# Tile-by-tile gather for the first expert, one-hot masks on ScalarE, two weight pieces decoded later

## The chip, the cores and the metric

The kernel runs on one core of one Trainium2 chip. The metric is device microseconds of one execution, the median of several runs. The engines are TensorE (PE in the profile, its weight loads PEld), VectorE (DVE), ScalarE (ACT), GpSimd (POOL) and SyncE (SP), whose queue issues nearly all DMAs.

## The reference

Three computations follow each other. The attention hashes queries and keys into 64 buckets by the signs of a projection on 6 columns, and masks pairs of different buckets. Its result, 1536 tokens of 512 numbers, goes to the one expert of eight with the highest logit. A last layer has a wide hidden vector of 1024 numbers, a softmax gate, a normalisation and an output product.

```python
mask = q_bucket[:, :, :, None] == k_bucket[:, :, None, :]
scores = np.where(mask, scale * np.matmul(q, k.transpose(0, 1, 3, 2)), -1000000000.0)
attn_out = softmax(scores) @ v                       # 2 x 8 heads x 768 x 64
x = attn_out as 1536 tokens x 512
e_idx = np.argmax(x @ w_gate, axis=1)
for e in range(8):
    ye = np.maximum(x[e_idx == e] @ w1[e], 0.0) @ w2[e]
    out[e_idx == e] = gate_w * eom * ye
h = out @ w_in; solu = h * softmax(h)
return normalise(solu) * g_ln @ w_out
```

`w_in` and `w_out` of the last layer arrive as 64-bit floats. The kernel reads them as pairs of 32-bit words and puts 32-bit floats together from these on the chip; this is called decoding here.

## The kernel before, in words

**Attention.** The order of instructions on each engine is the order in which the program emits them; nothing reorders it afterwards. 96 units of 128 queries x 768 keys pass through PE (scores), DVE (maximum), ACT (exponential), PE (transposes, product with v). Sixteen blocks `j` of three token tiles end in `fin_hi`, `fin_lo` (split of the result into two 16-bit halves), `fin_r` (reciprocal of the sums), `fin_mm` (PE: transposition and router logits), `fin_l` (logits to SBUF) and `fin_x` (tokens as two 16-bit halves `xh`; the second half of the split is on POOL, or on DVE for tile 11). L1028 to L1037 emit the units, and work in the background hangs on them by `at` and `due`.

**Routing.** Twelve token tiles are routed in five parts (L747): tiles 0 to 2, 3 to 5, 6 to 8, 9 and 10, and 11. `route_a` (L752, DVE) makes a one-hot row of the chosen expert for each token, `route_mm` (L771, PE) counts with small matmuls how many tokens of the same expert came before, `route_b` (L790) writes each token's slot `slot_f` on DVE and issues one indirect DMA per tile on POOL's queue, which scatters the tile's tokens into `xs` in DRAM. `route_s` (L810) adds the part's counts to `hs` on DVE, which the matmuls of later parts and of `totals` read.

**The gather for expert 0.** The other experts' tokens come back from `xs` by a transposing DMA (`x_load`, L1095). For expert 0 the tokens of tiles 0 to 5 are loaded so early (`gather_load`, L901), and the rest is put in by matmuls: `gather_first` (L925) writes the loaded rows into four PSUM tiles, `gather_oh` (L917) makes a mask of 128 x 224 per token tile on DVE (1 where the token's slot is the column), and `gather_mm` (L929) multiplies the tile's tokens by the mask, 8 matmuls per tile, six tiles. `gather_copy` (L937) moves the four PSUM tiles to SBUF with four copies on ACT. The order of all of this at the end of attention is written out by hand in L1040 to L1082; before, all six masks follow after the last parts are routed:

```python
for t in (6, 7, 8):
    oh(t)
    gm(t, range(4))
a_("route_b")(4)
for t in (9, 10, 11):
    oh(t)
    gm(t, range(4))
```

`totals` (L848) starts with one matmul of `hs`, ahead of the first expert's matmuls on PE, and goes on with a long series of small DVE operations that orders the experts by their number of tokens; from its `slot_i` SP reads into registers which weights to load (`expert`, L1212), and ACT and DVE read where results go. `route_d` (L819) makes the gate weights.

**Experts.** 64 slots of four per product (L1225 and on): `mm1` and `mm2` of eight experts with 24 matmuls each. `ev1` and `ev2` split a slot's result into a high half (ACT) and a low half (DVE, put off by one slot through `late`). A slot also has one piece of weights to split: ACT the high half (L167), DVE the low half (L171), with loads three slots ahead (`LA`) into five buffers `raw`. PSUM has eight buffers here, so PE can run some slots ahead of DVE.

**Decoding.** `w_in` and `w_out` are 16 pieces of 128 x 512. A piece takes a load (`wide_load`, L115), `wide_abs` on ACT, `wide_clamp` on POOL (L130), `wide_a`, `wide_c`, `wide_b` on DVE (L135, L141, L146), `wide_hi` on POOL (L152), `wide_lo` on DVE (L171). Pieces 0 to 2 are decoded during attention; the list `WD` (L1247) gives the slot at which each of pieces 3 to 15 starts, its load six slots before. In the list of before, piece 14 starts at slot 47 and piece 15 at 64, which is the first slot of the last stage.

**Last stage.** For token tile t = 0 to 11: `h2` (24 matmuls), `solu_a` to `solu_d` (softmax, normalisation, split, transposing DMA), and, from t = 4 on, `outp(t - 4)` (24 matmuls with `w_out`, then a scatter to the output). The work of slots 64 + 2t and 65 + 2t is emitted at the head of tile t.

Of the kernel before, what the change touches and what calls it, by code (L numbers as in the profile page):

```python
# [21 lines left out]
def kernel(  # L22
# [75 lines left out]
    win = const.tile([1, 4], I32, name="win")  # L98
    g1 = const.tile([128, KF], F32, name="g1")
    nhalf = const.tile([128, 1], F32, name="nhalf")  # L100


    wide = w_in.dtype == I64
# [155 lines left out]
    def setup_late():  # L259
        ie = const.tile([128, E], I32, name="ie")  # L260
        it = const.tile([128, B, NS], I32, name="it")
        g = nc.gpsimd
        g.memset(rg, 0.0)
        for h in range(2):
            r = slice(64 * h, 64 * h + 64)
            for wi, w in enumerate((w_gate, w_ogate)):
                c0 = 128 + 16 * h + 8 * wi
                nc.sync.dma_start(out=rg[r, :, c0 - 128:c0 - 120],
                                  in_=w.rearrange("(c h p) e -> h p c e", h=2, p=64)[h])
        nc.sync.dma_start(out=g1, in_=g_ln.rearrange("(f p) -> p f", p=128))  # L270
        g.iota(ie, pattern=[[1, E]], base=0, channel_multiplier=0)
        g.iota(it, pattern=[[S, B], [1, NS]], base=0, channel_multiplier=NS)
        make_upper_triangular(nc, upper, val=1.0, diag=False)
        g.memset(ones16, 1.0)
        g.memset(nhalf, -0.5)
        g.tensor_copy(out=iota8, in_=ie)
        g.tensor_copy(out=me[:, :, 1], in_=it.rearrange("p b s -> p (b s)"))
        g.tensor_scalar(out=iota_s, in0=iota8, scalar1=1.0 / 16.0, scalar2=1.0, op0=ALU.mult, op1=ALU.mult)
        g.tensor_scalar(out=ord0, in0=iota8, scalar1=-1.0, scalar2=1.0, op0=ALU.mult, op1=ALU.mult)
        for e in range(2):  # L280
            g.memset(ord0[:, e:e + 1], float(16 * NT * (2 - e)))
        for e in range(E):
            g.memset(caps[:, e:e + 1], float(CAPS[e]))
        for x in range(MW):
            g.memset(win_w[:, x:x + 1], float(WIN * x))
        g.tensor_scalar(out=row0, in0=iota8, scalar1=float(NT), scalar2=1.0, op0=ALU.mult, op1=ALU.mult)

        g.memset(hs, 0.0)
        g.tensor_scalar(out=hs[:, 0], in0=iota8, scalar1=float(NT // 128), scalar2=1.0, op0=ALU.mult, op1=ALU.mult)
# [20 lines left out]
    def attention(es):  # L310
# [603 lines left out]
                                    op0=ALU.add, op1=ALU.mult)  # L914
            gx["xe"], gx["oh"] = xe, bh

        def gather_oh(t):  # L917
            nc.vector.tensor_scalar(out=gx["oh"][:, t - 6], in0=gx["oh"][:, 6], scalar1=slot_f[:, t:t + 1],
                                    scalar2=None, op0=ALU.is_equal)

        def gather_ps():
            a = ps_s.tile([128, 2, 512], F32, tag="s", name="s")
# [13 lines left out]

        def gather_copy():  # L937
            xw = raw.tile([128, 1024], F32, tag="raw", name="raw").bitcast(F16)[:, 0:8 * CAP]
            xw = gx["xw"] = xw.rearrange("p (c n) -> p c n", c=8)
            for kk in range(4):  # L940
                nc.scalar.copy(out=xw[:, kk::4], in_=gx["ps"][kk][:, 0:2 * CAP].rearrange("p (a n) -> p a n", a=2))

        JL = 2 * NP - 2
        for n in range(1, NP):
# [66 lines left out]
    with tc.manual_schedule():  # L1011
        with ExitStack() as es:
            A = attention(es)
            pj = A["pj"]
            cm, rb, rg = A["cm"], A["rb"], A["rg"]
            setup_first()
            A["first"]()
            A["load"](1)
            setup_late()
            NU = A["NU"]  # L1020
            bg = A["bg"]
            JL = 2 * NP - 2
            a_ = A.__getitem__
            pv, fa, tr = a_("emit_pv"), a_("fin_a"), a_("emit_t")
            due = a_("due")
            J = JL + 1
            for i in range(NU):
                a_("emit_s")(i, a_("steps_t")(i - 2) if 2 <= i else iter(()))  # L1028
                due(i, 0)
                a_("emit_max")(i)  # L1030
                due(i, 1)
                if i == NU - 1:
                    tr(NU - 2)
                a_("emit_exp")(i)
                if i == 5 or i >= 6 and i % 2 == 0:
                    pv(i // 2 - 2)
                due(i, 2)  # L1037
            assert not bg, bg.keys()

            oh, gm = a_("gather_oh"), a_("gather_mm")  # L1040
            pv(NU // 2 - 2)
            a_("fin_l")(JL)
            a_("fin_x")(JL)
            a_("fin_r")(J, 0, 2)
            a_("fin_hi")(J, 0, 2, True)
            tr(NU - 1)
            a_("fin_lo")(J, 0, 2)
            a_("fin_mm")(J, 0, 2)
            a_("route_a")(2)
            pv(NU // 2 - 1)  # L1050
            a_("fin_hi")(J, 2, 3, True)
            a_("fin_l")(J, 0, 2)
            a_("fin_x")(J, 0, 2, True)
            a_("route_a")(3)
            a_("fin_lo")(J, 2, 3)
            a_("fin_r")(J, 2, 3)
            a_("gather_ps")()
            a_("gather_first")(range(4))
            a_("fin_mm")(J, 2, 3)
            a_("route_mm")(2, tail=True)  # L1060
            a_("route_b")(2)
            a_("fin_l")(J, 2, 3)
            a_("route_s")(2)
            a_("route_a")(4)
            a_("fin_x")(J, 2, 3, True, True)
            a_("route_mm")(3, tail=True)
            a_("route_b")(3)
            a_("route_mm")(4, (9, 10), True)
            for t in (6, 7, 8):
                oh(t)  # L1070
                gm(t, range(4))
            a_("route_b")(4)
            for t in (9, 10, 11):
                oh(t)
                gm(t, range(4))
            a_("gather_copy")()
            a_("route_s")(3)
            for x in range(3):
                a_("route_d")(x, 0, 1)
            a_("totals")()  # L1080
            for x in range(3):
                a_("route_d")(x, 2, 3, 4)  # L1082
# [12 lines left out]
        def x_load(e, r0, w=CAP):  # L1095
            xw = mp.tile([128, 2 * KD, CAP], F16, tag="xw", name="xw", bufs=3)
            x = nc.sync.dma_start_transpose(out=xw[:, :, 0:w], in_=xs[r0, :])
            xw_t[e] = xw
            if e in (1, "x"):
                for y in scattered:  # L1100
                    tc.add_manual_dep(x.ins, y.name, mybir.DependencyInfo(
# [55 lines left out]

        def mm1(e, g, n):
            w = wt["w1", e].rearrange("p a (k f) -> p a k f", k=KD)
            xw = xw_t[e][:, :, 0:n]  # L1160
            if g == 0:
                hh_t[e] = mp.tile([128, 2, KF, CAP], F16, tag="hh", name="hh")
            ps = ps_a.tile([128, 2, CAP], F32, tag="a", name="a")
            for i in range(2):
                fs = slice((2 * g + i) * 128, (2 * g + i + 1) * 128)
                for kk in range(KD):
                    nc.tensor.matmul(ps[:, i, 0:n], w[:, 0, kk, fs], xw[:, kk], start=(kk == 0), stop=False)  # L1167
                    nc.tensor.matmul(ps[:, i, 0:n], w[:, 0, kk, fs], xw[:, KD + kk], start=False, stop=False)  # L1168
                    nc.tensor.matmul(ps[:, i, 0:n], w[:, 1, kk, fs], xw[:, kk], start=False, stop=(kk == KD - 1))  # L1169
            return ps  # L1170

        def ev1(e, g, ps, n):
# [71 lines left out]
                f(*a)  # L1244


        WD = [0, 2, 6, 10, 14, 18, 22, 27, 32, 37, 42, 47, 64]  # L1247
        for x in range(16):
            if wide:
                if x < EARLY:  # L1250
# [206 lines left out]
```

## Time and profile before

| what | us |
|---|---|
| three runs, median (lowest to highest) | 526.81 (526.65 to 527.11) |
| the profiled execution, its own time | 526.2 |
| the profiled execution, its span | 524.4 |
| PE busy in the span | 501.5 (96%) |
| DVE busy | 389.5 (74%) |
| ACT busy | 317.4 (61%) |
| POOL busy | 283.2 (54%) |

The span runs from the first to the last instruction; 1.8 us of the profiled execution's own time lie outside it. Attention takes the span up to some 236 us, routing and gather to 251, the experts to 388, the last stage to the end. PE is busy nearly throughout, so what counts is where it waits or runs at its lower clock. In the timeline a row gives start, duration, engine, line and operation, the tile written and the tiles read, and in brackets how long the engine sat idle before it and what it waited for. A row "x4" stands for four like instructions.

### The profile page before, as it was taken

How to read it: one execution, taken by the hardware profiler on the slowest of the kernel's cores; microseconds unless marked ns; L12 is line 12 of the kernel's file. 1: busy time of each engine (PE TensorE's matmuls, PEld its weight loads, DVE VectorE, ACT ScalarE, POOL GpSimd, SP SyncE). 2: the span in 40 equal slices, each digit the busy share in tenths (PEclk: the TensorE clock that was granted, in tenths of full speed). 3: DMA queues.
4: the chain of work that ended last, by engine and by line, in shares of the span. 5: the costliest groups of instructions: out<-in, count | busy, mean ns of one | idle time of the engine just before them, and what ended most of it. 6: DMA issues, size and time to landing. Idle time of an engine off the chain costs nothing. (4 is left out here: it accounts for less than half of the span.)

```text
span 524.4 us, 12447 instructions
## 1 busy us (share of the span) xinstructions
PE 501.5 (96%) x4692; PEld 384.7 (73%) x4692; DVE 389.5 (74%) x926; ACT 317.4 (61%) x595; POOL 283.2 (54%) x433
## 2 busy tenths in 40 slices
PE   7799999999999999997999999999979999999994
PEld 4578787888787888886999999999854444444442
DVE  7788888888888888766489898969934887455610
ACT  5778787888778887881364665566612455334420
POOL 7999896969879796826166587212111012212131
PEclk9999999999999999998999999999999999999998
DMA  5678988763837675302699999998500236352250
GB/s 180 144 201 188 243 151 236 194 184 86 201 115 126 200 174 167 78 2 81 194 288 227 314 307 296 272 313 279 173 5 0 55 76 112 80 96 66 61 140 40
DMA packets 107183, 83.23 MB, mean 159 GB/s; under 512 B 80624, under 2 KB 89456, under 8 KB 107120
## 3 DMA queue, kind: packets, MB, share of 16 engines
q1 hardware_dynamic: 104816, 76.09, 57.8%
q0 software_dynamic: 2304, 6.31, 3.1%
q8 instruction: 38, 0.62, 0.5%
q14 instruction: 25, 0.20, 0.1%
HBM read 51.43 MB, written 9.97 MB: 117 GB/s over the span
## 5 line engine op out<-in xcount | busy, mean ns | idle before, releaser
L627 PE MATMUL t<-ident,p 128*128 128x128 f32 x576 | 126.1, 275 | 0.5
L615 ACT ACTIVATE p<-s,mx 128x768 f32<-128x768 f32 x96 | 95.7, 997 | 38.7 <-DVE mx L604 22.4
L600 DVE TENSOR_REDUCE mx<-s 128x1 f32<-128x768 f32 x96 | 91.6, 955 | 27.0 <-PE s L590 21.6
L629 ACT COPY pt<-t 128x384 f32<-128x384 f32 x192 | 85.5, 479 | 7.0 <-PE t L627 5.8
L627 PEld LDWEIGHTS t<-ident,p 128*128 128x128 f32 x576 | 77.8, 141 | 15.4 <-ACT pt L629 8.9
L651 PE MATMUL v<-pt,v 128*64 128x128 f32 x1128 | 72.0, 277 | 0.0
L1323 PE MATMUL h<-wi,yT 128*128 128x512 f16 x288 | 65.2, 386 | 2.9 <-PEq L1127 2.9
L651 PEld LDWEIGHTS v<-pt,v 128*64 128x64 f32 x1128 | 60.6, 137 | 7.8 <-issue 6.8
L1197 PE MATMUL a<-hh,wb 128*128 128x224 f16 (+5 forms) x256 | 63.4, 251 | 2.0 <-DVE hh L1176 1.9
L1391 PE MATMUL o<-wo,zT 128*128 128x512 f16 x288 | 63.6, 379 | 0.1
L130 POOL TENSOR_SCALAR dm<-dm 128x512 f32<-128x512 f32 x16 | 33.2, 2072 | 56.4 <-ACT dm L125 56.2
L1196 PE MATMUL a<-hh,wb 128*128 128x224 f16 (+5 forms) x256 | 63.4, 251 | 0.0
L1198 PE MATMUL a<-hh,wb 128*128 128x224 f16 (+5 forms) x256 | 63.4, 251 | 0.0
L590 PE MATMUL s<-k,q 128*128 128x384 f16 x192 | 59.0, 329 | 1.0 <-ACT p L615 1.0
L590 PE MATMUL s<-b,cm 128*128 128x384 f16 x192 | 57.2, 326 | 1.4 <-DVE b L552 1.4
L1323 PEld LDWEIGHTS <-yT 128*128 128x128 f16 x288 | 28.6, 99 | 38.0 <-issue 5.4
L1167 PE MATMUL a<-xw,wa 128*128 128x224 f16 (+5 forms) x224 | 55.2, 249 | 0.3 <-DVE hh L1176 0.3
L1169 PE MATMUL a<-xw,wa 128*128 128x224 f16 (+5 forms) x224 | 55.2, 249 | 0.0
L1168 PE MATMUL a<-xw,wa 128*128 128x224 f16 (+5 forms) x224 | 55.2, 249 | 0.0
L1391 PEld LDWEIGHTS <-zT 128*128 128x128 f16 x288 | 28.2, 98 | 34.3 <-issue 0.4
L1401 POOL DMA_INDIRECT out_dram<-o,tok x12 | 12.6, 1047 | 53.8 <-issue 46.9
L1339 ACT ACTIVATE ex<-h,st,csc 128x1024 f32<-128x1024 f32 x12 | 14.4, 1203 | 41.8 <-DVE st L1362 27.6
(269 smaller groups left out, 1031.4 us busy)
## 6 DMA issues: line engine op xcount, KB each, us to landing
raw<-in_moe_w_dram SPq DMA_DIRECT2D x64, 512.0 KB, 6.1
raww<-in_moe_w_in_dram SPq DMA_DIRECT2D x8, 512.0 KB
raww<-in_moe_w_out_dram SPq DMA_DIRECT2D x8, 512.0 KB
xs<-raw SPq DMA_DIRECT2D x8, 448.0 KB, 4.0
v<-in_v_dram SPq DMA_DIRECT2D x8, 384.0 KB
q<-in_q_dram SPq DMA_DIRECT2D x6, 384.0 KB
k<-in_k_dram SPq DMA_DIRECT2D x6, 384.0 KB, 5.6
cm<-q SPq DMA_DIRECT2D x14, 96.0 KB, 2.1
```

Source lines behind the costliest of these rows:

```text
L590: nc.tensor.matmul(t[:, c, 0:SB], d[x, h][:, s], flat(d[y, h])[:, c * SB:(c + 1) * SB], start=first, stop=not first)
L600: nc.vector.tensor_reduce(out=mx[:, 0:1], in_=t[:, :, 0:SB], op=ALU.max, axis=AX.XY)
L615: nc.scalar.activation(out=p, in_=s_t.pop(i)[:, :, 0:SB], func=AF.Exp, scale=mx[:, 1:2], bias=mx[:, 2:3], accum_out=sums[j][:, qt, h:h + 1])
L627: nc.tensor.transpose(t[:, g * 128:(g + 1) * 128], p[:, c, g * 128:(g + 1) * 128], ident)
L629: nc.scalar.copy(out=pt[i][:, 3 * c:3 * c + 3], in_=t[:, 0:SB].rearrange("p (g c) -> p g c", g=3))
L651: nc.tensor.matmul(o[64 * h:64 * h + 64], vt[:, h, c], ph[h][:, c], start=(c == 0), stop=(c == NS - 1), tile_position=(0, 64 * h))
L1167: nc.tensor.matmul(ps[:, i, 0:n], w[:, 0, kk, fs], xw[:, kk], start=(kk == 0), stop=False)
L1196: nc.tensor.matmul(ps, w[:, 0, f, ds], hh[:, 0, f], start=(f == 0), stop=False)
L1197: nc.tensor.matmul(ps, w[:, 0, f, ds], hh[:, 1, f], start=False, stop=False)
L1198: nc.tensor.matmul(ps, w[:, 1, f, ds], hh[:, 0, f], start=False, stop=(f == KF - 1))
L1323: nc.tensor.matmul(ps[:, c], yT[:, a, kk, ts], w_i[:, w, kk, c * 512:(c + 1) * 512], start=(kk == 0 and a == 0 and w == 0), stop=(kk == KD ...
L1391: nc.tensor.matmul(ps, zT[:, KF * a + f], w_o[:, w, f], start=(f == 0 and a == 0 and w == 0), stop=(f == KF - 1 and a == 1))
```

## The change

Five things are changed. (1) The hand-written order at the end of attention: `gather_ps`, `gather_first` and the matmuls of part 2 (`route_mm`) come ahead of `fin_mm` for tile 11, part 2's `route_b` comes ahead of `route_a(3)`, and each token tile's mask and matmuls follow soon after the tile is routed, among the routing of parts 3 and 4. (2) The masks of tiles 7 and 10 are made on ACT in two steps, as relu(1 - abs(slot - column)), with a constant `one` set on POOL at the start. (3) `gather_copy` writes another layout, in which each copy's 448 columns lie side by side, and two of its four copies are on DVE; since `route_s(3)` is emitted after it, these two DVE copies come ahead of `route_s(3)`, `route_d` and `totals` on DVE. (4) `mm1` and `x_load` index the tokens by the new layout. (5) In `WD`, piece 14 starts at slot 64 and piece 15 at slot 67, so both are decoded in the last stage; piece 14's load moves from slot 41 to 58, piece 15's from 58 to 61.

```diff
--- before.py
+++ after.py
@@ -98,6 +98,7 @@
     win = const.tile([1, 4], I32, name="win")
     g1 = const.tile([128, KF], F32, name="g1")
     nhalf = const.tile([128, 1], F32, name="nhalf")
+    one = const.tile([128, 1], F32, name="one")
 
 
     wide = w_in.dtype == I64
@@ -273,6 +274,7 @@
         make_upper_triangular(nc, upper, val=1.0, diag=False)
         g.memset(ones16, 1.0)
         g.memset(nhalf, -0.5)
+        g.memset(one, 1.0)
         g.tensor_copy(out=iota8, in_=ie)
         g.tensor_copy(out=me[:, :, 1], in_=it.rearrange("p b s -> p (b s)"))
         g.tensor_scalar(out=iota_s, in0=iota8, scalar1=1.0 / 16.0, scalar2=1.0, op0=ALU.mult, op1=ALU.mult)
@@ -914,9 +916,14 @@
                                     op0=ALU.add, op1=ALU.mult)
             gx["xe"], gx["oh"] = xe, bh
 
-        def gather_oh(t):
-            nc.vector.tensor_scalar(out=gx["oh"][:, t - 6], in0=gx["oh"][:, 6], scalar1=slot_f[:, t:t + 1],
-                                    scalar2=None, op0=ALU.is_equal)
+        def gather_oh(t, on_act=False):
+            o, i, sl = gx["oh"][:, t - 6], gx["oh"][:, 6], slot_f[:, t:t + 1]
+            if on_act:
+                y = pp.tile([128, 2, SB], F32, tag="p", name="y")[:, 0, 0:CAP]
+                nc.scalar.activation(out=y, in_=i, func=AF.Abs, scale=-1.0, bias=sl)
+                nc.scalar.activation(out=o, in_=y, func=AF.Relu, scale=-1.0, bias=one)
+            else:
+                nc.vector.tensor_scalar(out=o, in0=i, scalar1=sl, scalar2=None, op0=ALU.is_equal)
 
         def gather_ps():
             a = ps_s.tile([128, 2, 512], F32, tag="s", name="s")
@@ -936,9 +943,13 @@
 
         def gather_copy():
             xw = raw.tile([128, 1024], F32, tag="raw", name="raw").bitcast(F16)[:, 0:8 * CAP]
-            xw = gx["xw"] = xw.rearrange("p (c n) -> p c n", c=8)
+            gx["xw"] = xw.rearrange("p (k a n) -> p a k n", k=4, a=2)
             for kk in range(4):
-                nc.scalar.copy(out=xw[:, kk::4], in_=gx["ps"][kk][:, 0:2 * CAP].rearrange("p (a n) -> p a n", a=2))
+                o, i = xw[:, 2 * kk * CAP:2 * (kk + 1) * CAP], gx["ps"][kk][:, 0:2 * CAP]
+                if kk % 2:
+                    nc.vector.tensor_copy(out=o, in_=i)
+                else:
+                    nc.scalar.copy(out=o, in_=i)
 
         JL = 2 * NP - 2
         for n in range(1, NP):
@@ -1049,30 +1060,36 @@
             a_("route_a")(2)
             pv(NU // 2 - 1)
             a_("fin_hi")(J, 2, 3, True)
+            a_("gather_ps")()
+            a_("gather_first")(range(4))
+            a_("route_mm")(2, tail=True)
             a_("fin_l")(J, 0, 2)
             a_("fin_x")(J, 0, 2, True)
+            a_("fin_r")(J, 2, 3)
+            a_("fin_lo")(J, 2, 3)
+            a_("route_b")(2)
+            a_("fin_mm")(J, 2, 3)
+            oh(6)
+            oh(7, True)
+            oh(8)
+            a_("route_s")(2)
+            gm(6, range(4))
             a_("route_a")(3)
-            a_("fin_lo")(J, 2, 3)
-            a_("fin_r")(J, 2, 3)
-            a_("gather_ps")()
-            a_("gather_first")(range(4))
-            a_("fin_mm")(J, 2, 3)
-            a_("route_mm")(2, tail=True)
-            a_("route_b")(2)
+            gm(7, range(4))
+            a_("route_mm")(3, tail=True)
             a_("fin_l")(J, 2, 3)
-            a_("route_s")(2)
             a_("route_a")(4)
+            gm(8, range(4))
             a_("fin_x")(J, 2, 3, True, True)
-            a_("route_mm")(3, tail=True)
             a_("route_b")(3)
+            oh(9)
+            oh(10, True)
             a_("route_mm")(4, (9, 10), True)
-            for t in (6, 7, 8):
-                oh(t)
-                gm(t, range(4))
+            gm(9, range(4))
             a_("route_b")(4)
-            for t in (9, 10, 11):
-                oh(t)
-                gm(t, range(4))
+            oh(11)
+            gm(10, range(4))
+            gm(11, range(4))
             a_("gather_copy")()
             a_("route_s")(3)
             for x in range(3):
@@ -1095,7 +1112,7 @@
         def x_load(e, r0, w=CAP):
             xw = mp.tile([128, 2 * KD, CAP], F16, tag="xw", name="xw", bufs=3)
             x = nc.sync.dma_start_transpose(out=xw[:, :, 0:w], in_=xs[r0, :])
-            xw_t[e] = xw
+            xw_t[e] = xw.rearrange("p (a k) n -> p a k n", a=2)
             if e in (1, "x"):
                 for y in scattered:
                     tc.add_manual_dep(x.ins, y.name, mybir.DependencyInfo(
@@ -1157,16 +1174,16 @@
 
         def mm1(e, g, n):
             w = wt["w1", e].rearrange("p a (k f) -> p a k f", k=KD)
-            xw = xw_t[e][:, :, 0:n]
+            xw = xw_t[e][..., 0:n]
             if g == 0:
                 hh_t[e] = mp.tile([128, 2, KF, CAP], F16, tag="hh", name="hh")
             ps = ps_a.tile([128, 2, CAP], F32, tag="a", name="a")
             for i in range(2):
                 fs = slice((2 * g + i) * 128, (2 * g + i + 1) * 128)
                 for kk in range(KD):
-                    nc.tensor.matmul(ps[:, i, 0:n], w[:, 0, kk, fs], xw[:, kk], start=(kk == 0), stop=False)
-                    nc.tensor.matmul(ps[:, i, 0:n], w[:, 0, kk, fs], xw[:, KD + kk], start=False, stop=False)
-                    nc.tensor.matmul(ps[:, i, 0:n], w[:, 1, kk, fs], xw[:, kk], start=False, stop=(kk == KD - 1))
+                    nc.tensor.matmul(ps[:, i, 0:n], w[:, 0, kk, fs], xw[:, 0, kk], start=(kk == 0), stop=False)
+                    nc.tensor.matmul(ps[:, i, 0:n], w[:, 0, kk, fs], xw[:, 1, kk], start=False, stop=False)
+                    nc.tensor.matmul(ps[:, i, 0:n], w[:, 1, kk, fs], xw[:, 0, kk], start=False, stop=(kk == KD - 1))
             return ps
 
         def ev1(e, g, ps, n):
@@ -1244,7 +1261,7 @@
                 f(*a)
 
 
-        WD = [0, 2, 6, 10, 14, 18, 22, 27, 32, 37, 42, 47, 64]
+        WD = [0, 2, 6, 10, 14, 18, 22, 27, 32, 37, 42, 64, 67]
         for x in range(16):
             if wide:
                 if x < EARLY:
```

## Rows read from the trace of the kernel before

**Rows 1.** Windows by stage: us, busy time per engine, clock, DMA share, GB/s.

```profile
251.00:330.00 79.00, 79.00 (x846) 78.99 (x845) 68.05 (x134) 44.34 (x72) 45.32 (x40) 1.00 1.01 278
```

**Rows 2.** Timeline of PE, gather: start us, us, operation, idle before and releaser.

```profile
239.60 0.23 PE L706 MATMUL m<-rb,xt 128*128 128x160 f16 x1
...
240.41 0.18 PE L779 MATMUL v<-oh_all,upper 128*128 128x24 f16 x1
...
243.50 0.18 PE L779 MATMUL v<-oh_all,upper 128*128 128x8 f16 x1 [1.57 <-DVE rpr L797]
...
243.69 0.54 PE L934 MATMUL s<-raw,xh 128*128 128x224 f16 x4
...
249.18 0.55 PE L934 MATMUL s<-raw,xh 128*128 128x224 f16 x4
...
249.94 0.17 PE L852 MATMUL m<-hs,ones 128*128 128x8 f16 x1
250.82 0.26 PE L1167 MATMUL a<-raw,wa 128*128 128x224 f16 x1 [0.71 <-ACT raw L941]
```

**Rows 3.** Timeline of DVE over the same stretch.

```profile
238.94 0.16 DVE L758 TENSOR_REDUCE rmx<-lt 128x2 f32<-128x16 f32 x1
...
240.00 0.28 DVE L677 SCALAR_TENSOR_TENSOR xt<-s,xt 128x128 f16<-128x128 f32 x1
...
240.71 0.17 DVE L797 SCALAR_TENSOR_TENSOR rpr<-v,oh_all 128x8 f32<-128x8 f32 x1
...
240.97 0.19 DVE L718 TENSOR_TENSOR lt<-m,r 128x32 f32<-128x32 f32 x1
...
241.60 0.15 DVE L758 TENSOR_REDUCE rmx<-lt 128x1 f32<-128x8 f32 x1
...
242.33 0.28 DVE L731 TENSOR_TENSOR xf<-m,r 128x128 f32<-128x128 f32 x1
...
243.19 0.16 DVE L797 SCALAR_TENSOR_TENSOR rpr<-v,oh_all 128x8 f32<-128x8 f32 x1
...
243.36 0.93 DVE L918 TENSOR_SCALAR raw<-raw,slot_f 128x224 f16<-128x224 f16 x3
...
251.79 0.29 DVE L839 TENSOR_REDUCE rz<-rex 128x3 f32<-128x24 f32 x2 [6.15 <-ACT rex L833]
```

**Rows 4.** Timeline of ACT over the same stretch.

```profile
242.65 0.30 ACT L736 CAST xh<-xf 128x128 f16<-128x128 f32 x1 [3.10 <-DVE xf L731]
249.81 0.97 ACT L941 CAST raw<-s 128x448 f16<-128x448 f32 x2 [6.86 <-PE s L934]
```

**Rows 5.** Timeline of SP's queue after the gather.

```profile
255.89 2.49 SPq L181 DMA_DIRECT2D raw<-in_moe_w_dram  x3
```

**Rows 6.** Waits of PE in the expert stage: us, times, longest.

```profile
PE a L1197 <- DVE hh L1176: 1.9, 2, 1.0
...
PE a L1167 <- DVE hh L1176: 0.3, 1, 0.3
```

**Rows 7.** Timeline of PE around one of those waits.

```profile
372.35 0.24 PE L1196 MATMUL a<-hh,wb 128*128 128x184 f16 x1
373.54 0.24 PE L1197 MATMUL a<-hh,wb 128*128 128x184 f16 x1 [0.95 <-DVE hh L1176]
```

**Rows 8.** Windows of tile db alone, DVE: decode of piece 14.

```profile
371.80:375.70 3.90, 2.54 (x4) 1.00 0.79 262
```

**Rows 9.** Page, part 5: the clamp of the decode on POOL.

```profile
L130 POOL TENSOR_SCALAR dm<-dm 128x512 f32<-128x512 f32 x16 | 33.2, 2072 | 56.4 <-ACT dm L125 56.2
```

**Rows 10.** Timeline of DVE, last stage.

```profile
410.29 0.75 DVE L171 SCALAR_TENSOR_TENSOR wo<-db,g,wo 128x512 f16<-128x512 f32 x1
...
417.58 1.22 DVE L1336 TENSOR_REDUCE st<-h 128x1 f32<-128x1024 f32 x1
```

**Rows 11.** Timeline of PE, last stage.

```profile
418.60 5.34 PE L1391 MATMUL o<-wo,zT 128*128 128x512 f16 x24
```

**Rows 12.** Windows of PE in the gather: us, busy, clock, DMA share, GB/s.

```profile
245.00:246.00 1.00, 1.00 (x8) 0.50 0.50 201
```

## The prediction

> **What bounds the kernel now.** I went from the windows by stage to the waits of PE, and from each wait to the timelines of the engine it names. The windows show the expert stage with PE busy all the time and DVE busy 68 of 79 us, and the DMA engines full (share 1.01) [rows 1]: three candidates for a limit there. The waits show where PE loses time after the gather: twice for the low halves that DVE makes (`hh`), and once for a PSUM buffer that DVE frees, 2.2 us of idle time together [rows 6]. A wait costs more than its idle time, since the pipeline drains: the matmul at 373.54 starts 1.19 after the one before it, where 0.08 is usual, so 1.11 is lost for 0.95 of idle time [rows 7]. Three waits so cost 2.2 + 3 x 0.16 = 2.7 us.
>
> The other loss is the gather. PE is free for it at 239.60, when `gather_first` ends, and starts the first expert at 250.82 [rows 2]. In between, 48 gather matmuls begin only at 243.69, when all of the routing is done, after waits of which the longest is 1.57 [rows 2]. Then they take 243.69 to 249.94 = 6.25 us, though a tile's eight take 0.76 at the end (249.18 to 249.94), which makes 4.56 for six tiles [rows 2]. The 1.7 us of difference is the clock: in the window at 245 PE is busy throughout, with a granted clock of 0.50, the 1.2 GHz level, right after the stretch in which it mostly waited [rows 12]. After the gather, four copies on ACT, two of which take 0.97 [rows 4], hold the first expert until 250.82.
>
> **The change part by part.** Times are on the axis of the trace of before.
>
> *Order of the gather.* DVE's order is the same up to 238.94. Instead of `route_a(3)`, `fin_lo` and `fin_r` come next; they took 240.00 to 240.71 = 0.71, so they end at 239.65 [rows 3]. Part 2's `route_mm` starts at 239.60 instead of 240.41, and `route_b` can start 0.30 after it, as before (240.41 on PE, 240.71 on DVE): at 239.90, 0.81 earlier [rows 2, 3]. From there DVE is busy in one row: `route_b` 0.26 (240.71 to 240.97), masks 6 and 8 with 0.31 each at most (three in 0.93), `route_s` and `fin_l` 0.63 (240.97 to 241.60), `route_a(3)` 1.06 (238.94 to 240.00), `route_a(4)` 0.73 (241.60 to 242.33) [rows 3]. That is 3.30, so `fin_x` of tile 11 starts at 243.20, and `route_b(3)` 0.86 later, as before (242.33 to 243.19), at 244.06 [rows 3]. `route_mm(4)` reuses the PSUM tile that `route_b(3)` reads; it followed by 0.31 (243.19 to 243.50) and took 0.19 to the first gather matmul [rows 2, 3]. So tile 9's matmuls start at 244.56. By then tiles 6, 7 and 8 (3 x 0.76, from 240.5 on) are long done. Tiles 9, 10 and 11 follow without a gap if their masks are there, and tile 11's start at 246.08 instead of 249.18: 3.10 us gained.
>
> *Masks on ACT.* Two ACT operations in place of one on DVE. The trace has none of this shape: 0.30 for 128 columns and 0.49 for 448 (0.97 for two) are the nearest [rows 4], so 0.6 to 1.0 for a mask. I take 0.95, near the upper row, as the inputs are 224 wide and the second waits for the first. Mask 7, begun at 240.2 when its slots are known, then is ready at about 241.2, when tile 6's matmuls end, and mask 10 at 245.2, before 245.3, when PE asks for it: the matmuls of the tile before cover both, and without that cover each would cost 0.95. Behind them on ACT wait only the cast for tile 11 and the copies, which come later.
>
> *Copies.* They may start 0.63 after tile 11's matmuls begin (249.18 to 249.81) [rows 2, 4]: at 246.71. ACT does two in 0.97. DVE's are not in the trace: 0.28 for 128 columns is the lower and 0.75 for 512 the upper neighbour [rows 3, 10]; for 448 I take 0.6. But `route_s(3)` now stands behind them on DVE, and the matmul of `totals`, ahead of the first expert on PE (249.94, before 250.82) [rows 2], needs its counts. So PE waits for 246.71 + 1.2 + 0.3 (`route_s`) + 0.1 = 248.3, where the copies alone would let it go at 247.4. The first expert starts 2.5 us earlier. DVE's wait for ACT before 251.79 (6.15 idle) [rows 3] goes, as ACT is free at 247.7; six operations of about 0.14 put that point at 249.1, so `totals`, SP's first weight load (255.89) [rows 5] and DVE's part of the expert stage come 2.7 earlier or a little less. The scatters move 0.81 forward with `route_b` and keep their order on POOL; expert 1's rows are wanted 2.5 earlier. That may cost 0 to 1.7; I take 0, as [rows 6] have no wait for them.
>
> *Piece 14.* Its four DVE operations (2.54) [rows 8] leave the place just ahead of the late low halves. With 2.7 from the gather DVE is 5.2 earlier there, and PE, without its waits, wants the halves 2.5 + 2.7 = 5.2 earlier. I take 2.4 of the 2.7: the wait for PSUM comes before piece 14's work and shrinks only by the 0.2 that DVE gains on PE. The loads of pieces 14 and 15 move behind all weight loads on SP (the last is emitted at slot 52), so nothing is queued behind them there.
>
> *Last stage.* PE runs `h2` and `outp` back to back. Piece 14 takes the place that 15 had. For 15, POOL's clamp (2.07) [rows 9] stands ahead of the power that tile 0 waits for, DVE has 1.7 more of decoding in tile 2, and its `wide_lo` (0.75) [rows 10] goes ahead of the maximum at 417.58 [rows 10]: ready by 417.58 + 2.07 + 1.7 + 0.75 = 422.1. `outp(0)` starts at 418.60 and takes 5.34 for 24 matmuls [rows 11]; the last three alone use piece 15, from 423.2 on. Cost 0, with 1.1 us to spare; the constant `one` on POOL at the start: 0, at most 0.28, the smallest such row [rows 3].
>
> **Sum.** 2.5 + 2.4 = 4.9 us. The profiled execution would take 526.2 - 4.9 = 521.3; the median of before is 0.6 above it, so I forecast 521.9 us.
>
> **The rivals.** *A, the clock falls all the same.* PE still idles from about 243.1 to 244.4 and from 247.0 to 248.3. For it speaks that the clock fell after waits here [rows 12]; against it, that PE now works between 240.5 and 243. Price: the 1.7 us that before lost, 523.6. The Trainium skill, TensorE: Matmul & The Clock Gate, HAM oscillation, says that bursts of matmuls with waits between them pay again and again for the fallen clock; by that rule this is the outcome, and the 0.50 of [rows 12] agrees with it.
>
> *B, transfers set the expert stage.* Weights would then arrive as before and eat the early start. For it: the DMA share of 1.01 [rows 1]. Against it: PE's waits name DVE, not a load [rows 6], and loads wait for buffers that DVE frees. Only piece 14's 2.4 would be left: 524.4.
>
> *C, the last stage stalls.* DVE executes in order, and a decode step that finds POOL unready holds the next tile. One tile on DVE takes 7.29 - 0.75 = 6.5 (410.29 to 417.58) [rows 10]. If piece 15's `wide_lo` comes one such tile later than I put it, `outp(0)` waits 6.5 - 1.1 = 5.4, more than the gain: 527.3. It decides from 4.9 + 1.1 = 6.0 us of delay on. Against it: each POOL step has most of a tile's time to finish.
>
> **How the numbers follow.** The forecast has 0.60, B 0.18, A 0.13, C 0.05; 0.04 is for no effect. The range goes from 520.5 (narrow masks, DVE copies at their lower row, all of the 2.7) to 524.6, just past B; A lies within. A measurement of this kernel tells about 0.2% (1.05 us) from no change. Forecast, A and B are faster by more than that, less a little for mixtures of A and B: 0.89; same 0.05; slower 0.06.
>
> **What would show it.** Right: gather matmuls start near 240.5, tile 11's near 246.1, no 0.50 clock in the gather; the first expert's wait names DVE's counts, and it starts near 248.3; no `hh` waits of 0.9 near 372 and 382; the last stage without PE gaps. A wait of `outp` for `wo` in the last stage, or of ACT for loads that reaches PE, would make it wrong.

## The result, and the profile after

The changed kernel takes 521.47 us in the median (519.82 to 522.15, 4 runs), the kernel before beside it 526.96 (526.65 to 527.52, 4 runs): a ratio of 0.989, 95% interval 0.9865 to 0.9915. The forecast was 521.9, and the direction and the size hold. The sum behind it holds less well: the first expert's term is 0.3 smaller than forecast, piece 14's comes out between 1.6 and 2.8 from one execution to the next, and the clock in the last stage, which was not in the sum, gave 1.7 us in this profile.

The profiled execution has a span of 519.4 us against 524.4. Its axis lies 0.49 later than that of before when the gather starts (`gather_first` at 239.32, before 238.83), so the stretches are compared, not the times of day (in the other profiles with the new order the gather starts between 238.75 and 240.22):

| stretch, from first instruction to first instruction | before | after | gain |
|---|---|---|---|
| span's start to `gather_first` | 238.83 | 239.32 | -0.49 |
| `gather_first` to the first expert | 11.99 | 9.76 | 2.23 |
| first expert to the last stage | 140.19 | 138.55 | 1.64 |
| last stage's start to the first `outp` | 27.59 | 25.89 | 1.70 |
| first `outp` to the end | 105.80 | 105.88 | -0.08 |

The timeline of PE in the gather, the answer to [rows 2]:

```profile
240.08 0.18 PE L781 MATMUL v<-oh_all,upper 128*128 128x24 f16 x1
...
241.04 0.54 PE L941 MATMUL s<-raw,xh 128*128 128x224 f16 x4 [0.53 <-DVE raw L926]
...
244.63 0.18 PE L781 MATMUL v<-oh_all,upper 128*128 128x8 f16 x1 [1.05 <-DVE rpr L799]
...
244.86 0.54 PE L941 MATMUL s<-raw,xh 128*128 128x224 f16 x4
...
246.42 0.55 PE L941 MATMUL s<-raw,xh 128*128 128x224 f16 x4
...
249.06 0.17 PE L854 MATMUL m<-hs,ones 128*128 128x8 f16 x1 [1.71 <-DVE hs L817]
249.08 0.26 PE L1184 MATMUL a<-raw,wa 128*128 128x224 f16 x1
```

Less the 0.49, the gather matmuls begin at 240.55, tile 9's at 244.37, tile 11's at 245.93; the forecast had 240.5, 244.56 and 246.08. Then PE waits 1.71 for the counts (`hs`) that `totals` sums, and starts the first expert at 248.59 in place of the forecast's 248.3.

The timelines of DVE and ACT there, the answer to [rows 3, 4]:

```profile
240.38 0.17 DVE L799 SCALAR_TENSOR_TENSOR rpr<-v,oh_all 128x8 f32<-128x8 f32 x1 [0.32 <-PE v L788]
...
243.47 0.28 DVE L733 TENSOR_TENSOR xf<-m,r 128x128 f32<-128x128 f32 x1
...
247.57 0.62 DVE L950 CAST raw<-s 128x448 f16<-128x448 f32 x1 [2.08 <-ACT raw L952]
248.11 0.61 DVE L950 CAST raw<-t 128x448 f16<-128x448 f32 x1
248.64 0.17 DVE L816 TENSOR_REDUCE hn<-oh_all 128x8 f16<-128x24 f16 x1
248.84 0.16 DVE L817 TENSOR_TENSOR hs<-hs,hn 128x8 f16<-128x8 f16 x1
...
250.50 0.14 DVE L870 TENSOR_TENSOR tn<-m,row 128x8 f32<-128x8 f32 x1
```

```profile
240.75 0.48 ACT L923 ACTIVATE y<-raw,slot_f 128x224 f32<-128x224 f16 x1 [0.73 <-DVE rpr L799]
241.27 0.48 ACT L924 ACTIVATE raw<-y,one 128x224 f16<-128x224 f32 x1
...
247.00 0.53 ACT L952 CAST raw<-s 128x448 f16<-128x448 f32 x1 [1.40 <-PE s L941]
```

DVE's copies take 0.62 and 0.61, as estimated (0.6), but the first starts only at 247.57, 0.04 after ACT's first copy ends (247.00 + 0.53): the two did not start together. The profile puts DVE's wait on that copy, and in e3 below the two starts lie 0.57 apart as well (246.65 and 247.22); why the one waits for the other was not tested. The counts come behind both, at 248.64 and 248.84. A mask on ACT takes 1.0 us (240.75 to 241.27 + 0.48).

The waits of PE up to the last stage's start (to [rows 6]) and SP's queue (to [rows 5]):

```profile
PE h L1340 <- PEq L1144: 2.9, 1, 2.9
PE m L854 <- DVE hs L817: 1.7, 1, 1.7
PE a L1184 <- DVE hh L1193: 0.3, 1, 0.3
```

```profile
252.04 1.48 SPq L1114 DMA_TRANSPOSE xw<-xs  x1
254.95 2.52 SPq L182 DMA_DIRECT2D raw<-in_moe_w_dram  x3
```

Both `hh` waits of the second product (L1197 before) are gone; the PSUM wait stays at 0.34, where the forecast let it shrink by 0.2. Counted from `gather_first`, the first weight load comes 1.43 earlier (15.63, before 17.06), where 2.7 was forecast.

The windows of PE in the gather, first the kernel before, where 0.66 is a mean of the 2.4 GHz and the 1.2 GHz level, then the kernel after:

```profile
244.00:249.00 5.00, 5.00 (x38) 0.66 0.39 157
```

```profile
236.00:244.00 8.00, 6.95 (x86) 1.00 0.09 35
244.00:249.00 5.00, 2.72 (x28) 1.00 0.40 157
```

After the change the granted clock stays at 1.00, the 2.4 GHz level, though PE waits for 1.05 and 1.71 us in that stretch.

### The profile page after: what moved, and what is told of

Same layout as the page of the kernel before. It is cut to its first block, busy times and chain, and to the rows that moved or that the text cites. A ratio compares the mean times of both kernels' runs of the same rounds, so it can differ in the third digit from the quotient of the medians.

```text
span 519.4 us, 12453 instructions
## 1 busy us (share of the span) xinstructions
PE 498.6 (96%) x4692; PEld 383.1 (74%) x4692; DVE 389.5 (75%) x926; ACT 319.4 (61%) x597; POOL 283.7 (55%) x434
## 5 line engine op out<-in xcount | busy, mean ns | idle before, releaser
L1340 PE MATMUL h<-wi,yT 128*128 128x512 f16 x288 | 63.5, 379 | 2.9 <-PEq L1144 2.9
L168 ACT ACTIVATE wb<-raw 128x1024 f16<-128x1024 f32 x24 | 25.4, 1056 | 27.7 <-DMA raw<-in_moe_w_dram 27.5
```

What stands on the lines that cost most here:

```text
L1340: nc.tensor.matmul(ps[:, c], yT[:, a, kk, ts], w_i[:, w, kk, c * 512:(c + 1) * 512], start=(kk == 0 and a == 0 and w == 0), stop=(kk == KD ...
```

## The experiments

Each was timed beside the kernel before, with 6 to 12 runs. The stretches come from one profile each, out of its timeline of PE, as in the table above; "clock" is the mean over a kernel's runs of the granted clock, each over its whole span. e1 to e4, e5 to e8 and e9 to e12 ran beside the same runs of before each, whose medians were 526.41, 526.96 and 526.41 us.

| kernel | median us | ratio to before (95%) | gather | experts | to `outp` | clock |
|---|---|---|---|---|---|---|
| e1 pieces only | 523.74 | 0.994 (0.9918 to 0.9962) | 11.98 | 140.31 | 27.43 | 0.990 |
| e2 gather only | 523.83 | 0.9941 (0.9916 to 0.9965) | 9.77 | 141.35 | 25.90 | 0.994 |
| e3 counts first | 520.50 | 0.9894 (0.9867 to 0.9921) | 8.93 | 137.23 | 25.90 | 0.995 |
| e4 masks on DVE | 521.65 | 0.9919 (0.989 to 0.9948) | 9.99 | 137.38 | 27.59 | 0.994 |
| e5 changed, again | 521.99 | 0.9902 (0.9864 to 0.9941) | 9.76 | 138.46 | 27.45 | 0.994 |
| e6 fewer bytes | 521.86 | 0.9902 (0.9868 to 0.9937) | 9.77 | 139.02 | 25.90 | 0.994 |
| e7 three pieces | 521.98 | 0.9898 (0.9865 to 0.9931) | 9.76 | 137.45 | 28.77 | 0.994 |
| e8 totals first | 519.70 | 0.9857 (0.9824 to 0.989) | 8.70 | 137.45 | 25.90 | 0.994 |
| e9 before, filled | 524.25 | 0.9951 (0.9925 to 0.9976) | 10.59 | 139.81 | 27.34 | 0.994 |
| e10 totals first, filled | 520.15 | 0.9875 (0.9846 to 0.9905) | 8.72 | 138.51 | 25.90 | 0.996 |
| e11 loads first | 522.13 | 0.9938 (0.9912 to 0.9964) | 8.71 | 138.52 | 25.89 | 0.992 |
| e12 both | 522.59 | 0.992 (0.9895 to 0.9946) | 8.71 | 140.49 | 25.89 | 0.996 |

**The two halves of the change.** e1 is the kernel before with this edit, e2 the changed kernel with the list of before.

```diff
-        WD = [0, 2, 6, 10, 14, 18, 22, 27, 32, 37, 42, 47, 64]
+        WD = [0, 2, 6, 10, 14, 18, 22, 27, 32, 37, 42, 64, 67]
```

> The kernel before with the new list WD alone: pieces 14 and 15 start at slots 64 and 67, everything else as before. Theory 1 (the decode of piece 14 on DVE causes the two late low halves): the first expert starts as before near 250.8, the two waits of PE for hh of 0.95 us each near 372 and 382 are gone, the stretch from the first expert's first matmul to the last stage's first matmul shrinks from 140.2 to 137.8 to 138.3 us, the whole by 2 us to about 525. Theory 2 (the waits come from loads that are late for the whole stage): waits of hh of about the same sum stay, the stretch is 139.5 or more, the whole less than 1 us faster. Rival C (the last stage stalls): PE waits in the first outp for wo.

> The changed kernel with the old list WD (pieces 14 and 15 at slots 47 and 64). The first expert starts 2.2 us earlier than before, as in the changed kernel. Theory 1 (PE and DVE carry the early start through the expert stage): the two hh waits of 0.95 us stay as they are, the stretch of the experts is 140.2 us as before, the whole 2.2 us faster than before. Theory 2 (weight loads, which start only 1.4 us earlier, set the stage): the waits grow, the stretch is 140.6 to 141.2, and the whole gains 1.2 to 1.6 us. In both, a granted clock of 0.50 within the gather is gone.

Waits of PE, first e1 from the gather to the last stage, then e2 in the expert stage:

```profile
PE a L1167 <- DVE hh L1176: 2.0, 2, 1.6
```

```profile
PE a L1214 <- DVE hh L1193: 2.1, 2, 1.1
PE a L1184 <- DVE hh L1193: 0.3, 1, 0.3
```

With the pieces moved alone, the waits of the second product are gone, but in this execution PE met another, of 1.6 us for a PSUM buffer, so the stretch did not shrink; the runs gained 2.7 us all the same. With the gather alone, the waits stay, and the stretch is 1.2 longer than before: of the 2.2 us of earlier start 1.1 reach the end of the experts in this execution. The medians gain 2.7 and 2.6 us; the sum, 5.3, is about what the changed kernel gains. e1's profile alone would not have shown it: one execution scatters by 1 us and more in this stage (e4 and the changed kernel, whose code is alike from `totals` on, have 137.38 and 138.55).

**The counts.**

```diff
-            a_("gather_copy")()
             a_("route_s")(3)
+            a_("gather_copy")()
```

> The changed kernel with route_s(3) emitted ahead of gather_copy, so that the counts for the matmul of totals no longer stand behind two copies on DVE. Both theories: PE's wait of 1.7 us for hs is gone, and the first expert starts 1.1 to 1.3 us earlier, at about 0.6 us after the last gather matmul, waiting for the copies. Theory 1 (PE carries it): the whole is 1.1 to 1.3 us faster than the changed kernel, near 520.3. Theory 2 (loads set the expert stage, and they start after totals, which hardly move): the stretch of the experts grows by about as much, and the whole moves by less than 0.4 us.

```profile
246.45 0.55 PE L941 MATMUL t<-raw,xh 128*128 128x224 f16 x4
246.84 0.17 PE L854 MATMUL m<-hs,ones 128*128 128x8 f16 x1
```

In this timeline of e3 the matmul of `totals` follows the last gather matmuls at once. The first expert starts 0.83 earlier (8.93 for 9.76), less than expected, since PE then waits 0.9 for a DVE copy. The median is 520.50 against 521.47 and 521.99 for the changed kernel, and the stretch of the experts does not grow (137.23): the early start was carried, so theory 2 fails here. The difference in the medians is inside the intervals.

**The masks.**

```diff
-            oh(7, True)
+            oh(7)
...
-            oh(10, True)
+            oh(10)
```

> The changed kernel with the masks of tiles 7 and 10 on DVE again. If the two ACT masks help as the prediction has it, DVE's row is 2 x 0.2 to 0.3 us longer and the last gather matmuls start 0.2 to 0.6 us later; the first expert as much later. Rival: ACT masks (two steps of 0.48 us) are what tile 7 and tile 10 wait for, and with DVE's 0.3 us the gather ends at the same time or up to 0.3 us earlier. The whole moves by less than 0.6 us either way.

The first expert starts 0.23 later (9.99), so the masks on ACT are worth that much in these profiles, at the lower end of what was expected. In the whole time it cannot be seen.

**The changed kernel again.**

> The changed kernel itself, unchanged, beside the others on the same chip: how far its own runs and its own trace scatter. Both theories: the first expert 9.8 us after gather_first begins, the last gather matmuls 7.5 us after it; the stretch of the experts 137.2 to 139.5 us from execution to execution; the time from the first matmul of the last stage to the first outp either 25.9 us or, when the granted clock falls there, 27.6.

The windows of PE at the last stage's start, the first profile of the changed kernel, then this second one:

```profile
384.00:388.00 4.00, 1.09 (x12) 1.00 0.03 8
388.00:392.00 4.00, 4.00 (x21) 1.00 0.01 4
```

```profile
384.00:388.00 4.00, 0.85 (x3) 0.86 0.04 12
388.00:392.00 4.00, 4.00 (x15) 0.71 0.00 0
```

The same code, after the same wait of some 3 us: once the clock stayed at 1.00, once it fell, and the stretch to the first `outp` is 25.89 or 27.45. In the profile of before it fell (27.59). So 1.7 of the 5.0 us between the profiles of before and after is no effect that the code of the change explains. Of the twelve profiles here without extra matmuls at that place, before and after included, the clock fell in six, after waits of 2.88 to 3.31 us, and stayed in six, after 2.76 to 3.20: the length of the wait does not tell which.

**Fewer bytes.** On top of e2: pieces 6 to 13 take piece 5's words, which stay in a buffer of their own; the other pieces' loads have two buffers in place of three.

```diff
     def wide_load(x, pool):
+        if 6 <= x <= 13:
+            wide_t[x] = wide_t["kept"]
+            return
...
```

> The gather-only kernel (list WD of before), in which pieces 6 to 13 of the last stage's weights are not loaded: their decoding, all of its instructions, works on piece 5's words, so 8 loads of 512 KB are left out of the expert stage and the last stage's weights are wrong. Theory 1 (DVE's own work makes the low halves late): DVE has exactly the work it had, so PE's hh waits stay near 2 us and the stretch of the experts near 141. Theory 2 (DVE is late because splits and decoding wait for loads): ACT's waits for raw loads, 41 us in sum, shrink by a third or more, PE's hh waits fall under 0.7 us, and the stretch to 138 or less; the whole is 2 to 3 us faster than the gather-only kernel.

Waits of ACT for loads, first the gather-only kernel, then this one:

```profile
ACT wb L168 <- DMA raw<-in_moe_w_dram: 25.7, 14, 4.9
ACT wa L168 <- DMA raw<-in_moe_w_dram: 14.8, 11, 3.0
```

```profile
ACT wb L174 <- DMA raw<-in_moe_w_dram: 26.3, 15, 4.6
ACT wa L174 <- DMA raw<-in_moe_w_dram: 13.9, 12, 2.5
```

40.5 and 40.2 us: 4 MB less to load did not shorten ACT's waits. PE's `hh` waits fell from 2.4 to 1.3, the stretch from 141.35 to 139.02, the median by 2.0 (across two sets of runs). Neither theory fits. Loads may have a part in DVE's lateness, but not as theory 2 has it; how it comes about stays open, and with one profile each and intervals that overlap the part itself is not certain.

**Three pieces in the last stage.**

```diff
-        WD = [0, 2, 6, 10, 14, 18, 22, 27, 32, 37, 42, 64, 67]
+        WD = [0, 2, 6, 10, 14, 18, 22, 27, 32, 37, 64, 65, 67]
```

> The changed kernel with a third piece moved into the last stage (pieces 13, 14, 15 start at slots 64, 65, 67). It doubles what rival C suspects. In the changed kernel the low half of piece 15 is ready 1.4 us before the first outp asks for it; a third piece puts 2.5 us of DVE work and a clamp of 2 us on POOL ahead of it. If the cover is as thin as that, PE waits 1 to 3 us for wo in the first outp, and the last stage grows by as much, while the expert stage loses at most the 0.3 us of waits it has left: slower than the changed kernel by 1 to 3 us. If the last stage has more room than I think, no wait for wo appears and the whole is the same within 0.5 us.

Timeline of PE in e7, the first `outp`:

```profile
415.14 4.91 PE L1408 MATMUL o<-wo,zT 128*128 128x512 f16 x22
420.30 0.59 PE L1408 MATMUL o<-wo,zT 128*128 128x512 f16 x2 [0.24 <-DVE wo L172]
```

PE waits after 22 of 24 matmuls, at the very place that rival C named, but for 0.24 us; the median is that of the changed kernel. In this execution the clock had fallen, for longer than in the others, and the first `outp` began 2.9 us later, which may hide some more. So the cover is thin, and a third piece uses it up, at a price too small to see.

**Totals first.** The counts, `route_d` and `totals` ahead of the copies, which are all on ACT:

```diff
...
-            a_("gather_copy")()
             a_("route_s")(3)
             for x in range(3):
                 a_("route_d")(x, 0, 1)
             a_("totals")()
+            a_("gather_copy")()
```

> The changed kernel with route_s(3), route_d and all of totals emitted ahead of gather_copy, and the four copies on ACT again, so that nothing of the copies stands on DVE. The first expert waits for two copies on ACT alone, 1.6 us after the last tile's matmuls begin: 0.6 to 0.9 us earlier than in the changed kernel. SP's registers come about 3 us earlier, but SP first issues the transposing load of expert 1's rows, which waits for the last scatter, so the first weight load moves by 1 us at most. Theory 1 (PE carries the start): 0.6 to 0.9 us faster than the changed kernel. Theory 2 (loads and DVE set the expert stage): DVE's part begins 2 us or more earlier, since its registers no longer wait, the loads 1 us; the hh wait that is left goes, and the whole is 0.8 to 1.5 us faster.

```profile
248.09 0.17 PE L854 MATMUL m<-hs,ones 128*128 128x8 f16 x1
248.92 0.26 PE L1181 MATMUL a<-raw,wa 128*128 128x224 f16 x1 [0.67 <-ACT raw L949]
```

The first expert starts 1.06 earlier than in the changed kernel (8.70 for 9.76), without DVE's copies, and no `hh` wait is left; but e4's and e7's profiles, with `totals` behind the copies, have none either. The first weight load does not move: it comes 15.63 after `gather_first`, as in the changed kernel, though `totals` goes on 3.1 earlier. At 519.70 it is the fastest: 2.3 below the changed kernel beside it. At equal clock over the run it is faster too: 519.65 against 522.23 and 521.75 at 0.993, 518.41 against 520.51 and 519.44 at 0.997. It beats the kernel before clearly (0.9857); its interval and the changed kernel's (0.9864 to 0.9941) overlap.

**The clock in the gather.** The kernel before with idle time filled:

```diff
+            if i == 3:
+                for _ in range(26):
+                    nc.tensor.matmul(m[:, 128:256], ident16, ident16, start=True, stop=True)
             rmm[i] = m
```

> The kernel before, with 26 extra matmuls of 128 columns (1.4 us of work, written to PSUM columns that nobody reads) behind the counts of part 3, where PE waits 1.57 us for DVE. The order of the gather, masks, copies and pieces are those of before. Theory 1 (much of the gather's gain is the clock, which falls after PE's waits): the granted clock stays at 1.00 in the gather, its 48 matmuls take 4.6 to 4.8 us in place of 6.3, the first expert starts 1.5 to 1.7 us earlier, the mean clock of the runs rises by 0.003, the whole gains 1.3 to 1.7 us. Rival (the earlier order itself is what counts, the clock is set by what came long before): the 0.50 stays, and the first expert starts where it did.

Windows of PE in e9 over the stretch of the fence with 0.66 above, and its timeline:

```profile
242.00:244.00 2.00, 1.65 (x30) 1.00 0.32 131
244.00:249.00 5.00, 4.71 (x50) 1.00 0.39 157
```

```profile
241.78 1.61 PE L790 MATMUL v<-ident 128*128 128x128 f16 x26
...
243.95 0.54 PE L937 MATMUL s<-raw,xh 128*128 128x224 f16 x4
...
248.54 0.17 PE L855 MATMUL m<-hs,ones 128*128 128x8 f16 x1
```

Nothing but useless work was added, and the clock stays up: the 48 gather matmuls take 4.59 in place of 6.25, so the low clock had cost 1.66. The extra matmuls put their start off by 0.26, and the first expert starts 1.40 earlier (10.59 for 11.99). The runs gain 2.2 us in the median (0.9951), their mean clock goes from 0.991 to 0.994. The rival falls. So over half of the 2.23 us that the changed gather gains is to be had without any of its new order.

**Filling the second wait.** On top of e8:

```diff
         run_late()
+        w = ps_a.tile([128, 2, CAP], F32, tag="a", name="a").rearrange("p a n -> p (a n)")
+        for _ in range(14):
+            nc.tensor.matmul(w, ident16, wt["wi", 0][:, 0, 0:2 * CAP], start=True, stop=True)
         overflow()
```

> The kernel with totals first and all copies on ACT, and with 14 extra matmuls of 448 columns (2.7 us of work, into a PSUM tile that nobody reads) after the last expert, in front of the branch on the overflow count, where PE waits 3 us for its sequencer. Theory 1 (the clock falls at the start of the last stage after this wait, in some executions): the fall there is gone in the profile and in the runs, the clock of all runs is 0.996 or 0.997, the first matmul of the last stage starts where it did, as the extra work runs while the sequencer waits; against the kernel with totals first the median gains 0.5 to 1.2 us and the runs scatter less. Rival: PE's sequencer waits for its queue to empty, and the last stage starts 2.5 us later: slower by 1.5 to 2.5 us.

The timeline of PE:

```profile
382.08 2.81 PE L1322 MATMUL a<-wi,ident 128*128 128x448 f16 x14
386.51 8.79 PE L1340 MATMUL h<-wi,yT 128*128 128x512 f16 x40 [1.62 <-DVE db L136]
```

In this profile, and in that of e12, the granted clock stays at 1.00 into the last stage. No run's clock over the whole span is below 0.994, where e8's go down to 0.990. That the fall is gone in every run is not shown: one fall is worth about 0.003 there (0.996 and 0.993 in the two profiles of the changed kernel), so a run at 0.994 may have one. The runs scatter less, 519.36 to 520.67 against 518.30 to 520.51 for e8, but the median is no better (520.15 against 519.70, in another set of runs). The rival is right in part: counted from the experts' last matmul, the last stage starts 1.07 later than in e8, and in e12 1.60 later than in e11, which has no extra matmuls. That is about what a fall costs, so nothing is gained.

**Loads first.** On top of e8 (e12: on top of e10):

```diff
-        x_load(1, slice(NT, NT + CAP))
...
             if prep[x]:
                 w_load(*prep[x])
+            if x == 5:
+                x_load(1, slice(NT, NT + CAP))
```

> The kernel with totals first, in which SP issues two weight loads of expert 2 ahead of the transposing load of expert 1's rows instead of behind it. The first weight load moves 2 to 3.5 us forward. Theory 2 (loads set the expert stage): the waits of ACT for raw loads and the hh waits shrink, and the whole gains 0.5 to 1.5 us against totals first alone. Theory 1 (PE carries the start, and its expert stage is already without waits): no change within 0.4 us. Against both: expert 1's rows come late and PE waits for them at the ninth microsecond of the first expert, up to 2 us.

> Totals first, extra matmuls ahead of the last stage, and the two weight loads ahead of expert 1's rows, together. If each does what it is for: 518 us or less in the median, faster than the changed kernel by 3 us or more. If the extra work delays the last stage or expert 1's rows come late, it shows in the same places as in the kernels with one of the two.

SP's queue in e11 and a wait of PE:

```profile
251.10 1.00 SPq L182 DMA_DIRECT2D raw<-in_moe_w_dram  x2
252.43 2.46 SPq L1111 DMA_TRANSPOSE xw<-xs  x1
```

```profile
PE a L1181 <- DMA xw<-xs: 1.4, 1, 1.4
```

The first weight load comes 4.2 earlier than in e8, counted from `gather_first`. PE now waits 1.4 for expert 1's rows (1.7 in e12), and without that wait the stretch would be 137.1, hardly less than e8's 137.45. So an earlier start of the loads shows no gain here, where no `hh` wait was left that it could shorten; with the list of before, which has such waits, it was not tried. The late rows cost: both kernels are slower than e8, by 2.4 and 2.9 us in the medians (across two sets of runs), more than these two waits explain. e12, expected at 518 or less, took 522.59.

## Why the prediction was right, point by point

*The gather's order.* Right, and step for step: the matmuls of tiles 6, 9 and 11 came within 0.2 us of their forecast, masks on ACT took 1.0 (0.95) and were covered. What the gain of 3.25 us in the start of the last tile's matmuls is made of, e9 lets one estimate: 1.66 is the clock, which no longer falls, and the other 1.59 the order. Both were in the sum, as one number.

*The copies.* That PE would wait for the counts behind DVE's copies was forecast, at 0.9 us; e3, with the counts ahead, starts 0.83 earlier. The term for the first expert is 2.23 in place of 2.5: from the last tile's matmuls to the first expert pass 2.66 us, where the forecast has 2.22, since the two engines' first copies ran one after the other (247.00 and 247.57), where I had let them start together.

*Piece 14.* The mechanism was right: the two late low halves are in all four profiles with the list of before (before, e2, e6, e9) and in none of the ten with its work moved. The size is not settled. The stretch of the experts is 1.64 and 1.73 shorter in the two profiles of the changed kernel, 2.81 in that of e4, which has the same code from `totals` on, and e1's runs gain 2.7 with the list alone; 2.4 was forecast. The changed kernel's two profiles have the PSUM wait of 0.34, e4's has not. What did not come as written is that `totals`, "SP's first weight load" and DVE's part "come 2.7 earlier or a little less": `totals` does (L870 at 250.50, 2.67 earlier from `gather_first`), but the load only 1.43, as it stands behind the transposing load that waits for the last scatter; and of the early start with the old list (e2) just 1.1 of 2.2 reached the end. That loads which start late cause this is not shown: e11 moved them 4.2 us forward for nothing, but had no late low half left, and e6 took 4 MB of them away and got part of the gain.

*The last stage.* "Cost 0, with 1.1 us to spare" was right. Piece 15's low half was ready at 416.14 + 0.75 = 416.9, and the first `outp`, from 413.52 on, wanted it near 418.2: 1.3 to spare.

```profile
416.14 0.75 DVE L172 SCALAR_TENSOR_TENSOR wo<-db,g,wo 128x512 f16<-128x512 f32 x1
```

*The sum.* The two terms measure 2.23 + 1.64 = 3.9 us in the profile, in place of 4.9 (4.0 with the second profile's stretch, 5.0 with e4's). That the profiled execution took 521.17 where 521.3 was forecast is luck: 1.70 of its gain is the clock at the last stage's start, which the sum did not hold and which falls there in some executions of both kernels. The medians too owe a part to the clock. In e5's set the mean clock is 0.994, that of before 0.989; 0.005 over 525 us is 2.6 us of PE's time, an estimate, of which the gather, inside the 2.23, accounts for about 1.7. Runs of about equal clock differ by less than the medians' 5.0: at 0.990 the changed kernel has 523.91 against 525.32 and 526.35, at 0.991 522.88 against 525.73, at 0.993 521.75 and 522.23 against 523.33 at 0.994, so 1 to 3 us. That fits the terms, which come to 2.2 without the gather's clock. Runs of before that go from 523.33 to 529.07 also show that a difference of 0.2% is less than such a measurement tells.

*The rivals.* A was wrong: none of the profiles with the new order has a clock under 1.00 in the gather, although PE waits there for about 1.1 and, in the changed kernel, 1.71. The fall that it expects came at the last stage's start instead, in some executions. B was wrong in its form: with the new list, the early start reached the end of the experts in e3 and e8; with the old one, in e2's profile, half of it did. C did not come about; e7 shows that it names the right place.

## What to carry to other kernels

A gap on the busiest engine costs its length and, in some executions, the clock behind it: before reordering work to close one, fill it with useless matmuls in an experiment, which tells how much of the gain is the clock's. When work is moved to an engine that is idle at the moment, look at what is emitted behind it there: here two copies put a tiny count, and with it PE, 0.8 us late (e3). And where runs of one kernel scatter by 2 us, as here, compare stretches of several profiles and runs of equal granted clock before a gain of that size is credited to an edit.

## What the runs showed of the hardware that I had not expected

After the same wait of about 3 us ahead of the last stage, the granted clock fell in six of twelve profiles and not in the others. A fall cost 1.4 to 1.7 us, and 2.9 in e7, where the low clock lasted longest; with extra matmuls in that wait it stayed up in both profiles (e10, e12). In e10 the 14 extra matmuls took 2.81 us but put the last stage off by 1.07 only (1.60 in e12), so part of this queued work was done while PE would have waited at the branch. And leaving out 4 MB of loads in a stage whose DMA share is 1.00 (e2, 250 to 330 us) did not shorten the waits for the loads that were left (40.5 and 40.2 us).
